# Pairs' matrix products from seven products of halves instead of eight, with weights in rings of quarters

## The chip, the cores and the metric

The kernel runs on one core of a Trainium2 chip. The metric is the device time of one launch in microseconds. The program works with five engines that run their own instruction streams: TensorE (PE; its weight loads are shown apart as PEld), VectorE (DVE), ScalarE (ACT), GpSimd (POOL) and SyncE (SP), and with DMA queues. Order between engines comes from semaphore waits that the framework puts in for every true dependence, overwriting included.

## The reference

A block of cross attention between 512 tokens and 32 state rows is followed by a mixture of 8 experts with top-1 routing. Input: `x` (8, 8, 512, 64) and `state` (8, 8, 32, 64); after attention, 8 x 544 = 4352 rows of width 512.

```python
# attention: x reads the states, the states read x, both softmaxed
xread = softmax(scale * x @ state.T) @ state
sread = softmax(scale * state @ x.T) @ x
rows  = concat([xread, sread], axis=2)         # -> (8, 544, 512)
# routing, row by row of one batch
fresh_e = argmax(rows @ w_gate)
e = fresh_e if s == 0 or sigmoid(rows @ w_local) < 0.5 else prev_e
p = softmax(rows @ w_gate)
# expert e of 8: w1 is 512 x 1024, w2 is 1024 x 512
h = maximum(row @ w1[e], 0)
out = p[e] * (h @ w2[e])
```

All of it is float32.

## The kernel before

The program has three stages: attention (class `Attention`), routing (class `Routing`), and the experts (function `experts`, from line 745). The change is in the last one, with small edits to what the routing allocates.

Routing sorts the rows by expert. Every expert's rows are cut into *pairs* of 2 x 128 rows (`PAIR` = 256), and what is left of each expert into *tiles* of 32 rows. With the inputs of this case there are 16 pairs and 10 tiles. How many there are is known only at run time; at least 10 pairs exist whatever the data (`NPMIN`), so the first nine calls of `pair` stand in straight code, and from the tenth on each pair asks in a branch (function `last`, line 937) whether another follows. Pairs 0 to 9 each carry one tile along (`tiles[u]`), the later ones none.

A pair u does this (function `pair`, line 859):

- SyncE loads the weights of pair u+1: `load`, four pieces of 1 MB, halves of w1 into `a` and of w2 into `c`. Both exist twice and are used in turn (line 752).
- VectorE turns the rows of pair u+1 (`turned`, line 778: two block transposes of 128 x 512 from `xg` into `xt`), GpSimd fetches those of pair u+2 (`gather`, line 767: eight indirect DMAs of quarter rows).
- First layer: for pairs from 1 on, 8 blocks of 128 hidden units by 4 steps of the 512-wide sum, each a matmul with a 128 x 128 block of w1 held in the array and 256 columns of rows streamed (line 875). ScalarE takes each full PSUM bank through the ReLU into `h` (line 877). Pair 0 does the same for 128 rows at a time, so its matmuls stream 128 columns (line 886).
- `tile.one` (line 832): the tile's first layer, 32 rows held and 256 columns of w1 streamed at a time, ReLU on ScalarE, transpose on VectorE.
- `after.load(0)` and `after.gather`: w1 of the next tile into `at`, its rows.
- Second layer, for each 128 rows: 8 matmuls with a block of `h` held and 512 columns of w2 streamed (line 902). VectorE multiplies by the rows' probability into `y` (line 906) and GpSimd scatters `y` into `out` with an indirect DMA (line 908).
- `tile.two` (line 845): the tile's second layer, scaled on VectorE (854), scattered by GpSimd (856). Then `after.load(1)`: w2 of the next tile into `ct`, and `after.turned`.

The order of the work is the order of the code (`tc.manual_schedule`): every engine and every queue runs its instructions in the order in which the calls above issue them, and waits where a dependence is open. SyncE's queue holds all weight loads, so a load that waits for its buffer holds back the loads behind it. GpSimd's queue holds gathers and scatters. [...]

Of the kernel before, what the change touches and what calls it, by code (L numbers as in the profile page):

```python
# [18 lines left out]
P = 128  # L19
# [30 lines left out]
def kernel(  # L50
# [24 lines left out]

    nc = tc.nc
# [29 lines left out]
    with ExitStack() as phase:  # L106
        bank = banks(phase, 7)
        route.route(bank, phase, lt, slots)
        experts(phase, tc, bank, w1, w2, rows, slots, route, out)
# [344 lines left out]
class Routing:  # L454
# [79 lines left out]
    def route(self, bank, ctx, lt, slots):  # L534
# [3 lines left out]
        idle = ctx.enter_context(self.tc.tile_pool(name="idle", bufs=1, space=PSUM)).tile([P, 512], F32, name="idle")  # L538

        def keep(n):  # L540

            for i in range(n):
                nc.tensor.matmul(idle, lhsT=identb, rhs=place.rearrange("p k c -> p (k c)"),
                                 start=True, stop=True)
# [123 lines left out]
        bc = rt.tile([P, 2, NG, NBLK, CG], BF16, name="bc")  # L668
# [48 lines left out]
        def probabilities():  # L717
# [3 lines left out]
            pb = rt.tile([P, 3, NG, NBLK, CG], BF16, name="pb")  # L721
# [23 lines left out]
def experts(ctx, tc, bank, w1, w2, rows, slots, route, out):  # L745
# [3 lines left out]
    hp = ctx.enter_context(tc.tile_pool(name="hp", bufs=2))  # L749


    as_ = [[fx.tile([P, KT, F // 2], F32, name=f"a{i}{h}") for h in range(2)] for i in range(2)]
    cs_ = [[fx.tile([P, FK // 2, D], F32, name=f"c{i}{h}") for h in range(2)] for i in range(2)]
    at_ = fx.tile([P, KT, F], F32, name="at")
    ct_ = fx.tile([P, FK, D], F32, name="ct")
    xts_ = [fx.tile([P, KT, PAIR], F32, name=f"xt{i}") for i in range(2)]
# [3 lines left out]
    first = [fx.tile([P, D], F32, name=f"first{b}") for b in range(2)]  # L760
# [17 lines left out]
    def turned(u):  # L778
        for b in range(2):
            x_t = xts_[u % 2][:, :, b * P:b * P + P]  # L780
            if u:
                nc.vector.transpose(x_t.rearrange("p k (i t) -> p k i t", i=Q),  # L782
                                    xgs_[u % 2][:, b].rearrange("p i k t -> p k i t"))
                continue

            for h, copy in enumerate((nc.vector.tensor_copy, nc.scalar.copy)):
# [4 lines left out]
                copy(x_t[:, 2 * h:2 * h + 2, :], t.rearrange("p (k t) -> p k t", k=KT // 2))  # L791
# [5 lines left out]
    def load(u, parts=range(4)):  # L797
        e = index(slots.experts[0:1, u - 1:u] if u else slots.expert if 0 in parts else slots.again)
        for i in parts:
            to, w = ((as_, w1), (cs_, w2))[i // 2]  # L800
            to, w = to[u % 2][i % 2], w[bass.ds(e, 1), i % 2]
            if u == 0 and i < 2:
                chunks = w.rearrange("o (q x) (k f) -> (o x) k q f", q=Q, k=KT)
                for j in range(KT):
                    nc.sync.dma_start(out=to[SQ * j:SQ * j + SQ], in_=chunks[:, j])
# [3 lines left out]
    class Tile:  # L809
# [12 lines left out]
        def load(self, of):  # L822
            e = index(slots.experts[0:1, NP - 1 + self.i:NP + self.i])
            for half in range(2):
# [3 lines left out]
                else:  # L828
                    to = ct_[:, half * FK // 2:(half + 1) * FK // 2, :].rearrange("p m d -> p (m d)")
                    nc.sync.dma_start(out=to, in_=w2[bass.ds(e, 1), half].rearrange("o p x -> (o p) x"))  # L830
# [14 lines left out]
        def two(self):  # L845

            yps = bank(P, P)
            for m in range(FK):
                for g in range(Q):
                    nc.tensor.matmul(yps[SQ * g:SQ * g + SQ, :], lhsT=self.h[:, m, :], rhs=ct_[:, m, g * P:g * P + P],  # L850
# [7 lines left out]

    def pair(u, ahead=True, tile=None, after=None):

        a, c, x_t = as_[u % 2], cs_[u % 2], xts_[u % 2]
        if ahead:
            load(u + 1)
            if u:
                turned(u + 1)
        if ahead and u and u + 2 < NP:
            gather(u + 2)
        h = hp.tile([P, FK, PAIR], F32, name="h")
        if u:
            for n in range(4):  # L870
                hps = bank()
                for i in range(2):
                    f = (2 * n + i) % 4 * P
# [123 lines left out]
```

## Time and profile before

| | us |
|---|---|
| median of 10 runs (629.26 to 632.7) | 630.65 |
| the profiled execution | 630.79 |
| its span, first to last instruction | 629.0 |
| TensorE busy | 583.8 (93%) |
| VectorE busy | 155.2 (25%) |
| ScalarE busy | 95.6 (15%) |
| GpSimd busy | 217.4 (35%) |
| mean granted TensorE clock of the core | 0.974 |

The experts' stage starts at 125.7 us, where pair 0's first matmul runs, and TensorE's last matmul ends at 614.2. In the timeline a line is: start, length, engine, line of the kernel, operation, what it writes <- what it reads, count, and in brackets how long the engine sat idle before it and who ended that. A busy TensorE is modelled from the matmuls' ends, so two starts that lie apart by a whole group are the better measure of what a group costs. "PEld" is the loading of the held operand, which overlaps the matmuls. In a group's row, the first number behind the bar is the time in which at least one of its instructions ran, the second the mean length of one in ns; lengths overlap.

### The profile page before, as it was taken

To read this page: it belongs to the slowest core of one execution; us is meant where nothing else is said; L and a number is where in the kernel's file an instruction comes from. 1 tells how busy PE (TensorE), PEld (TensorE's weight loads), DVE (VectorE), ACT (ScalarE), POOL (GpSimd) and SP (SyncE) were. 2 spreads that over 40 slices of the span, in tenths; PEclk is the share of its full clock that TensorE was granted. 3 is DMA by queue.
4 is the path that set the end of the run, shared out by engine and by line. 5 is a ranking of instruction groups with operands and counts; after the bars stand their busy time and mean duration, and the time that the engine had idled before them with its cause. 6 is when DMAs were issued, how large, how long until landed. Compare 5 with 4: busy or idle time off the path is not lost. (4 is left out here: it accounts for less than half of the span.)

```text
span 629.0 us, 9298 instructions
## 1 busy us (share of the span) xinstructions
PE 583.8 (93%) x3760; PEld 379.8 (60%) x3763; DVE 155.2 (25%) x335; ACT 95.6 (15%) x190; POOL 217.4 (35%) x218
## 2 busy tenths in 40 slices
PE   7678776799999999999999999999999999999990
PEld 3455552495757575757575766666667585766750
DVE  4698988721101010101010101010101011010000
ACT  5446531210010101010101010101011010101100
POOL 4333430373151616151515151516154151433000
PEclk9889997799999999999999999999999999999996
DMA  8968732699995969695959595959597355550000
GB/s 321 410 217 290 264 142 93 153 350 403 351 374 226 383 227 384 216 392 213 395 207 395 209 398 208 395 205 398 208 408 263 133 222 192 207 181 23 35 21 20
DMA packets 43227, 159.35 MB, mean 253 GB/s; under 512 B 8049, under 2 KB 8177, under 8 KB 31394
## 3 DMA queue, kind: packets, MB, share of 16 engines
q1 hardware_dynamic: 35682, 140.04, 59.7%
q0 software_dynamic: 7488, 18.56, 8.2%
q8 instruction: 35, 0.57, 0.4%
q14 instruction: 22, 0.18, 0.1%
HBM read 140.74 MB, written 17.96 MB: 252 GB/s over the span
## 5 line engine op out<-in xcount | busy, mean ns | idle before, releaser
L902 PE MATMUL ps<-c,h 128*128 128x512 f32 x512 | 223.4, 594 | 0.0
L875 PE MATMUL ps<-xt,a 128*128 128x256 f32 x960 | 210.7, 380 | 0.0
L875 PEld LDWEIGHTS ps<-xt,a 128*128 128x128 f32 x960 | 181.6, 190 | 28.4 <-issue 4.4
L902 PEld LDWEIGHTS ps<-c,h 128*128 128x128 f32 x512 | 96.5, 190 | 119.2 <-issue 118.7
L764 POOL DMA_INDIRECT xg<-rows,row x128 | 124.8, 975 | 39.0 <-issue 38.1
L908 POOL DMA_INDIRECT out_dram<-y,tok x32 | 32.2, 1008 | 201.5 <-DVE y L906 195.7
L877 ACT ACTIVATE h<-ps 128x512 f32<-128x512 f32 x60 | 35.8, 597 | 402.1 <-PE ps L875 402.1
L906 DVE TENSOR_SCALAR y<-ps,prob 128x512 f32<-128x512 f32 x32 | 24.0, 751 | 272.3 <-PE ps L902 272.3
L436 PE MATMUL v<-sd,a 128*128 128x265 f32 x128 | 34.7, 405 | 12.6 <-ACT xr L439 9.0
L843 DVE STREAM_TRANSPOSE htt<-ht 128x256 f32<-128x256 f32 x10 | 4.5, 445 | 132.4 <-ACT ht L841 132.4
L436 PEld LDWEIGHTS v<-sd,a 128*128 128x128 f32 x128 | 22.4, 189 | 23.2 <-ACT xr L439 15.1
L856 POOL DMA_INDIRECT out_dram<-yt,row x10 | 9.8, 981 | 73.3 <-issue 73.3
L387 POOL TENSOR_TENSOR e<-e,z 128x1024 f32<-128x1024 f32 x8 | 15.3, 1912 | 28.2 <-DVE z L386 28.2
L375 POOL TENSOR_TENSOR e<-e,m 128x1024 f32<-128x1024 f32 x8 | 15.3, 1912 | 17.5 <-DVE m L374 17.5
L850 PEld LDWEIGHTS ps<-ct,htt 128*32 128x32 f32 x640 | 16.9, 110 | 6.9 <-issue 6.8
L850 PE MATMUL ps<-ct,htt 128*32 128x128 f32 x640 | 19.5, 274 | 0.0
L838 PE MATMUL ps<-at,xtt 128*32 128x256 f32 x320 | 19.3, 382 | 0.0
L782 DVE STREAM_TRANSPOSE xt<-xg 128x512 f32<-128x512 f32 x30 | 19.1, 674 | 0.0
L886 PE MATMUL ps<-xt,a 128*128 128x128 f32 x128 | 14.5, 276 | 0.6 <-DVE experts L720 0.6
L344 PE MATMUL s<-x_t,sttc 64*32 64x512 f32 x128 | 12.7, 715 | 2.5 <-issue 2.1
L886 PEld LDWEIGHTS ps<-xt,a 128*128 128x128 f32 x128 | 14.4, 192 | 0.8 <-DVE again L719 0.8
L838 PEld LDWEIGHTS ps<-at,xtt 128*32 128x32 f32 x320 | 9.4, 109 | 8.4 <-issue 3.3
(178 smaller groups left out, 301.3 us busy)
## 6 DMA issues: line engine op xcount, KB each, us to landing
c<-in_w_dram SPq DMA_DIRECT2D x32, 1024.0 KB, 17.2
a<-in_w_dram SPq DMA_DIRECT2D x30, 1024.0 KB, 10.3
at<-in_w_dram SPq DMA_DIRECT2D x22, 1024.0 KB, 7.6
ct<-in_w_dram SPq DMA_DIRECT2D x22, 1024.0 KB, 8.6
x_t<-in_xt_dram SPq DMA_DIRECT2D x16, 512.0 KB, 7.1
x_n<-in_xn_dram SPq DMA_DIRECT2D x8, 1024.0 KB, 8.2
rows<-xr SPq DMA_DIRECT2D x8, 1024.0 KB, 5.7
a<-in_w_dram SPq DMA_DIRECT2D x8, 256.0 KB, 7.6
```

The source lines that it names most:

```text
L375: nc.gpsimd.tensor_tensor(e1, e1, m1.to_broadcast([P, A, N]), op=Alu.subtract)
L436: nc.tensor.matmul(v[:, u, :VW], lhsT=self.a[:, u, c * P:c * P + P], rhs=at.sd[:, b, u * VW:(u + 1) * VW], start=True, stop=True)
L764: nc.gpsimd.indirect_dma_start(out=to.rearrange("p k t -> p (k t)"), out_offset=None, in_=rows.rearrange("n q x -> (n q) x"), in_offset=ba ...
L782: nc.vector.transpose(x_t.rearrange("p k (i t) -> p k i t", i=Q), xgs_[u % 2][:, b].rearrange("p i k t -> p k i t"))
L838: nc.tensor.matmul(hps[SQ * g:SQ * g + SQ, :], lhsT=self.x_t[:, j, :], rhs=a[:, j, :, g], start=(j == 0), stop=(j == KT - 1))
L850: nc.tensor.matmul(yps[SQ * g:SQ * g + SQ, :], lhsT=self.h[:, m, :], rhs=ct_[:, m, g * P:g * P + P], start=(m == 0), stop=(m == FK - 1))
L875: nc.tensor.matmul(hps[:, i * PAIR:(i + 1) * PAIR], lhsT=a[n // 2][:, j, f:f + P], rhs=x_t[:, j, :], start=(j == 0), stop=(j == KT - 1))
L877: nc.scalar.activation(h[:, 2 * n:2 * n + 2, :].rearrange("p m t -> p (m t)"), hps, Act.Relu)
L886: nc.tensor.matmul(hps[:, i * P:i * P + P], lhsT=a[n][:, j, i * P:i * P + P], rhs=x_t[:, j, of], start=(j == 0), stop=(j == KT - 1))
L902: nc.tensor.matmul(yps, lhsT=h[:, m, b * P:b * P + P], rhs=c[m // 4][:, m % 4, :], start=(m == 0), stop=(m == FK - 1))
L906: nc.vector.tensor_scalar(y, yps, slots.prob[:, k:k + 1], None, Alu.mult)
L908: nc.gpsimd.indirect_dma_start(out=out, out_offset=to, in_=y, in_offset=None, bounds_check=NT - 1, oob_is_err=False)
```

## The change

For pairs from 1 on, both layers are cut into 2 x 2 blocks, and each layer's eight block products become seven (Strassen's algorithm in Winograd's form), with sums of blocks before and after. Written for weights a (blocks a11, a12, a21, a22) and rows b:

- `first_sums` and `second_sums` make three sums of weight blocks in free ring slots and overwrite a fourth block (a21, or w2's b12) with a fourth sum: four additions of 128 x 1024 on VectorE for each layer. `column_sums` makes four sums of the rows' blocks (128 x 256).
- `seven` issues the products in the order 1, 5, 6, 2, 7, 3, 4. The product 1 goes into a rotating bank `x`; ScalarE copies it into a bank of its own, `y` (one of the two `sums`), and the products 6, 7 and 4 add to that bank by further matmuls without a new start. Product 2 adds to `x`, product 3 to `v`, where 5 stands. Between the products ScalarE takes the partial sums out to SBUF (`s5, s2, s7`; in the second layer `r5, r2, r7`, scaled by the rows' probability), and VectorE adds them up.
- The first layer's results stay as four blocks (`h11, h21, c12, h22`), and VectorE makes the four sums that the second layer's products need from them (`hs`, and `c12` in place).
- A product of the first layer is 8 matmuls with 128 x 128 held and 128 columns streamed; one of the second layer is 4 matmuls with 256 columns streamed.

Weights lie in two rings of nine slots of 512 KB (`ring`), one for w1 and one for w2; a pair takes seven slots of each, four for quarters and three for sums, and the next pair's quarters begin in the two slots behind them. So of the four quarters of a layer two are loaded at the start of the pair before, and two after its product 2, where `others` issues them. w2 is laid out by quarters in DRAM on the host (a reshape of the input). Rows have one buffer `x_t` instead of two; the sums and the transpose for the next pair (`ready`) are issued after product 2 of the second layer.

Pair 0 (`plain`) keeps its products, with the second layer in halves of 256 columns. The first pair's w1 is loaded in 16 pieces instead of 8. The tile's transpose moves from the end of a pair to the start of the next, behind `second_sums`. The rotating banks are six, and the routing's `keep` matmuls go to the two `sums` banks in turn. The loads ahead of pair 0 are issued in the order w2 of pair 0, `at`, w1 of pair 1, `ct`, w2 of pair 1.

```diff
-        bank = banks(phase, 7)
+        bank = banks(phase, 6)
+        sums = phase.enter_context(tc.tile_pool(name="sums", bufs=1, space=PSUM))
+        sums = [sums.tile([P, 512], F32, name=f"sum{i}") for i in range(2)]
...
+    RING = 9
+    ring = [[fx.tile([P, KT // 2, F // 2], F32, name=f"a{i}") for i in range(RING)],
+            [fx.tile([P, FK // 2, D // 2], F32, name=f"c{i}") for i in range(RING)]]
...
+    first = [fx.tile([P, D], F32, name=f"y{b}") for b in range(2)]
+    ys = first
+    xs = [fx.tile([P, KT // 2, P], F32, name=f"xs{i}") for i in range(4)]
+    hs = [fx.tile([P, FK // 2, P], F32, name=f"hs{i}") for i in range(3)]
+    h11, h21, c12, h22 = hqs = [fx.tile([P, FK // 2, P], F32, name=f"h{i}") for i in range(4)]
+
+    def places(u, i):
+        n = 7 * u - 3 if u else 0
+        (w11, w12, w21, w22), sums = [[ring[i][(n + j) % RING] for j in js] for js in (range(4), range(4, 7))]
+        return ((w11, w12), (w21, w22)) if i == 0 else ((w11, w21), (w12, w22)), sums
...
+    def load(u, i, quarters=slice(4)):
+        e = index(slots.experts[0:1, u - 1:u] if u else slots.again if i else slots.expert)
+        q = places(u, i)[0]
+        for half, other in [((0, 0), (0, 1), (1, 0), (1, 1)), ((0, 0), (1, 0), (0, 1), (1, 1))][i][quarters]:
+            to = q[half][other]
...
+            if u == 0 and i == 0:
...
+                    nc.sync.dma_start(out=to[SQ * j:SQ * j + SQ], in_=chunks[:, j, 2 * other:2 * other + 2])
...
+    def add(out, a, b, op=Alu.add):
+        nc.vector.tensor_tensor(out, a, b, op=op)
+
+    def sums_of_rows(x, to, third):
+        (b11, b12), (b21, b22) = x
+        add(to[0], b12, b11, Alu.subtract)
+        add(to[1], b22, to[0], Alu.subtract)
+        third(b22, b12)
+        add(to[2], b21, to[1], Alu.subtract)
+
+    xq = [[x_t[:, 2 * j:2 * j + 2, t * P:t * P + P] for t in range(2)] for j in range(2)]
+
+    def first_sums(u, part):
+        ((a11, a12), (a21, a22)), to = places(u, 0)
+        if part == 0:
+            add(to[0], a21, a22)
+            add(to[1], to[0], a11, Alu.subtract)
+        else:
+            add(a21, a11, a21, Alu.subtract)
+            add(to[2], a12, to[1], Alu.subtract)
+
+    def column_sums():
+        sums_of_rows(xq, (xs[0], xs[1], xs[3]), lambda b22, b12: add(xs[2], b22, b12, Alu.subtract))
+
+    def second_sums(u):
+        sums_of_rows(*places(u, 1), lambda b22, b12: add(b12, b12, b22, Alu.subtract))
+
+    def seven(y, n, product, copies, whole):
+        x, v = bank()[:, :n], bank()[:, :n]
+        y = y[:, :n]
+        product(x, 1, True)
+        nc.scalar.copy(y, x)
+        product(v, 5, True)
+        five, two, three = copies
+        five(v)
+        product(y, 6)
+        two(y)
+        product(x, 2)
+        whole(1, x)
+        product(y, 7)
+        three(y)
+        whole(4, None)
+        product(v, 3)
+        whole(2, v)
+        product(y, 4)
+        whole(3, y)
...
+    def strassen(u, others, between, ready):
...
+        firsts = {1: (a11, b11), 2: (a12, b21), 3: (was[2], b22), 4: (a22, xs[3]), 5: (was[0], xs[0]),
+                  6: (was[1], xs[1]), 7: (a21, xs[2])}
+        s5, s2, s7 = [h1.tile([P, FK // 2, P], F32, name=f"s{i}") for i in range(3)]
...
+        def first(to, i, begin=False):
+            w, x = firsts[i]
+            for m in range(FK // 2):
+                for j in range(KT // 2):
+                    nc.tensor.matmul(to[:, m * P:m * P + P], lhsT=w[:, j, m * P:m * P + P], rhs=x[:, j, :], ...)
+
+        def first_whole(i, t):
+            if i == 1:
+                others(0)
+                nc.scalar.activation(flat(h11), t, Act.Relu)
+            elif i == 4:
+                add(flat(h22), flat(s7), flat(s5))
+                nc.scalar.activation(flat(h22), flat(h22), Act.Relu)
+            elif i == 2:
+                add(flat(c12), t, flat(s2))
+                nc.vector.scalar_tensor_tensor(hs[0], c12, 0.0, h22, Alu.max, Alu.add)
+                add(hs[1], hs[0], h11, Alu.subtract)
+                nc.vector.scalar_tensor_tensor(c12, c12, 0.0, h11, Alu.max, Alu.subtract)
+            else:
+                nc.scalar.activation(flat(h21), t, Act.Relu)
+                add(hs[2], h21, hs[1], Alu.subtract)
...
+        between()
...
+        seconds = {1: (h11, d11), 2: (h21, d21), 3: (hs[2], d22), 4: (h22, wcs[2]), 5: (hs[0], wcs[0]),
+                   6: (hs[1], wcs[1]), 7: (c12, d12)}
...
+        def second_whole(i, t):
+            if i == 1:
+                others(1)
+                scaled(ys[0][:, low], p0)(t)
+                ready()
+            elif i == 4:
+                add(ys[1][:, high], r7, r5)
+            elif i == 2:
+                nc.vector.scalar_tensor_tensor(ys[0][:, high], t, p0, r2, Alu.mult, Alu.add)
+                scatter(2 * u, ys[0])
+            else:
+                scaled(ys[1][:, low], p1)(t)
+                scatter(2 * u + 1, ys[1])
...
+    def pair(u, ahead=True, tile=None, after=None):
+        if u:
+            if ahead:
+                for i in range(2):
+                    load(u + 1, i, slice(2))
+                if u + 2 < NP:
+                    gather(u + 2)
+            second_sums(u)
+            if tile:
+                tile.turned()
+
+        def between():
+            if u == 0:
+                next(route.probabilities)
+            if tile:
+                tile.one()
+            if after:
+                after.load(0)
+                after.gather()
+            if u == 0:
+                gather(2)
+
+        def others(i):
+            if ahead:
+                load(u + 1, i, slice(2, 4))
+
+        def ready():
+            if ahead:
+                first_sums(u + 1, 0)
+                turned(u + 1)
+                column_sums()
+                first_sums(u + 1, 1)
+
+        if u:
+            strassen(u, others, between, ready)
+        else:
+            plain(u, between, ready)
...
         if tile:
             tile.two()
         if after:
             after.load(1)
-            after.turned()
...
-    load(0, range(2, 4))
-    for of in range(2):
-        tiles[0].load(of)
+    load(0, 1)
+    tiles[0].load(0)
+    load(1, 0)
+    tiles[0].load(1)
+    load(1, 1)
```

138 lines of the change are left out of this document (66 added, 72 removed).

## Prediction

> **What bounds the kernel now.** I read the page from the top, then the groups, then TensorE's timeline, then each stage's window, and only then the queues that the change touches.
>
> ```profile
> span 629.0 us, 9298 instructions
> PE 583.8 (93%) x3760; PEld 379.8 (60%) x3763; DVE 155.2 (25%) x335; ACT 95.6 (15%) x190; POOL 217.4 (35%) x218
> PE   7678776799999999999999999999999999999990
> ```
>
> TensorE is full in every slice from the ninth on, which is the experts' stage. The groups and the timeline tell what one pair costs; first pair 0, whose first layer streams 128 columns at a time, then the others.
>
> ```profile
> L875 PE MATMUL ps<-xt,a 128*128 128x256 f32 x960 | 210.7, 380 | 0.0
> L886 PE MATMUL ps<-xt,a 128*128 128x128 f32 x128 | 14.5, 276 | 0.6 <-DVE experts L720 0.6
> L886 PEld LDWEIGHTS ps<-xt,a 128*128 128x128 f32 x128 | 14.4, 192 | 0.8 <-DVE again L719 0.8
> ```
>
> ```profile
> 125.72 14.53 PE L886 MATMUL ps<-xt,a 128*128 128x128 f32 x128 [0.61 <-DVE experts L720]
> 140.09 5.67 PE L687 MATMUL ps<-pb,inp 128*128 128x150 bf16 x40
> ```
>
> ```profile
> 416.98 14.08 PE L875 MATMUL ps<-xt,a 128*128 128x256 f32 x64
> 430.99 1.93 PE L838 MATMUL ps<-at,xtt 128*32 128x256 f32 x32
> 432.86 14.00 PE L902 MATMUL ps<-c,h 128*128 128x512 f32 x32
> 446.79 1.96 PE L850 MATMUL ps<-ct,htt 128*32 128x128 f32 x64
> 448.67 14.08 PE L875 MATMUL ps<-xt,a 128*128 128x256 f32 x64
> ...
> 476.32 13.98 PE L875 MATMUL ps<-xt,a 128*128 128x256 f32 x64
> 490.14 13.90 PE L902 MATMUL ps<-c,h 128*128 128x512 f32 x32
> 503.87 13.98 PE L875 MATMUL ps<-xt,a 128*128 128x256 f32 x64
> ```
>
> Each float32 matmul of the code is two passes in the trace (32 matmuls, x64). Group L875 holds 960/64 = 15 pairs, u = 1 to 15. Nine of them carry a tile of 32 tokens and take 448.67 - 416.98 = 31.69 us; the six later ones take 503.87 - 476.32 = 27.55: 13.82 for the first layer, 215.9 ns a pass of 256 columns, and 13.73 for the second, 429.1 ns a pass of 512. In these six nothing idles between the groups. So the stage is bound by the columns that TensorE streams.
>
> ```profile
> 125.70:140.20 14.50, 14.47 (x129) 14.50 (x130) 3.33 (x4) 1.79 (x3) 11.55 (x10) 1.00 0.94 344
> 163.50:177.50 14.00, 14.00 (x72) 12.07 (x68) 1.76 (x4) 1.79 (x3) 4.94 (x6) 1.00 0.98 382
> 478.00:506.00 28.00, 28.00 (x99) 18.64 (x99) 3.17 (x5) 2.39 (x4) 10.09 (x11) 1.00 0.53 189
> ```
>
> In these windows (columns: length, busy PE, PEld, DVE, ACT, POOL, clock, DMA share, GB/s) the granted clock is 1.00, so there is no clock to win or lose. Vector works 3 us of 28 and Scalar 2.4: room for additions.
>
> **The change, part by part.** *Products.* A first-layer product of halves is 4 x 2 matmuls of 128 columns, 16 passes; a second-layer one is 4 matmuls of 256 columns, 8 passes. Seven of each make 112 passes of 128 and 56 of 256. For the second I take 215.9 ns: 12.09 us. For the first the right row is pair 0, which already streams 128 columns with a fresh weight tile each time: (140.09 - 125.72)/128 = 112.3 ns, so 12.58 us and 1.80 us a product. Below that lies half of the 256-wide pass, 108.0 ns; above, the L886 group's own 14.5/128 = 113.3. A pair falls from 27.55 to 24.67 us, by 2.88; fifteen give **-43.2 us**, with 2.77 to 3.37 a pair from the two ends, -41.5 to -50.5. Pair 0 keeps its eight products; its second layer becomes 64 passes of 256, 13.82 us against 13.73, nothing.
>
> *Additions.* Their prices:
>
> ```profile
> L391 DVE STREAM_TRANSPOSE a<-e 128x1024 f32<-128x1024 f32 x8 | 9.7, 1209 | 0.0
> L637 DVE TENSOR_TENSOR at<-at,less 128x320 f32<-128x320 f32 x1 | 0.5, 470 | 0.0
> L681 DVE TENSOR_TENSOR inp<-place,pos 128x1024 bf16<-128x1024 bf16 x4 | 2.5, 685 | 0.0
> L375 POOL TENSOR_TENSOR e<-e,m 128x1024 f32<-128x1024 f32 x8 | 15.3, 1912 | 17.5 <-DVE m L374 17.5
> L791 DVE COPY xt<-ps 128x256 f32<-128x256 f32 x2 | 0.8, 425 | 1.4 <-PE ps L790 1.4
> L782 DVE STREAM_TRANSPOSE xt<-xg 128x512 f32<-128x512 f32 x30 | 19.1, 674 | 0.0
> L877 ACT ACTIVATE h<-ps 128x512 f32<-128x512 f32 x60 | 35.8, 597 | 402.1 <-PE ps L875 402.1
> ```
>
> No row is a float32 add of 1024 on Vector. The bfloat16 one (0.69) lies below, GpSimd's float32 one (1.91) above. The transposes give 535 ns for 512 elements more, so 0.47 us at 320 becomes 1.2 at 1024; I take that. 512 elements cost 0.7, 256 cost 0.43. Per pair: eight weight sums, 9.6; four column sums, 1.7; six steps on the first layer's results, 4.2; two on the second's, 0.9; the transposes as before, 1.3; together 17.7 us, a tile's three steps 1.1 more. That is 72% of 24.67 (at 1.91 an add it would be 23.4, 95%). Scalar gets seven moves of 512 (0.6) and six of 256 (taken as 0.43 too): 6.8 us. Both fit under TensorE, if their results come in time.
>
> Do they? The order is 1, 5, 6, 2, 7, 3, 4. The first bank is copied while product 5 runs (0.6 us and a handover against 1.80), and each later copy has a product between it and the matmul that adds to the same bank. The second layer's product 5 needs the sum made from product 3: three Vector steps, 2.1 us, against product 4, 1.80, and product 1, 1.73. The sums for the next pair (the calls in `ready`) stand in Vector's queue behind the last first-layer step, at about 14 us of a pair, and take 7.9 (four adds, transposes, column sums): done at 22, or 23 in a tile pair, where TensorE wants them at 24.7 and 28.8. `second_sums` then takes 4.8 and is wanted 12.6 later. Between products waits are added, 14 a pair, but satisfied ones cost nothing in the rows: 490.14 - 476.32 is exactly 64 passes with three groups' boundaries inside. If they were not satisfied, TensorE itself would stand.
>
> *Moved.* A tile's transpose (0.3 us on Vector) goes from the end of a pair to behind `second_sums`, 7 us before `tile.one` wants it; `gather(2)` moves within GpSimd's queue from before to behind a tile's gather, wanted a pair later. Of six banks instead of seven a pair takes two for each layer and two for its tile, so each comes round a pair later. All three: nothing, and about their own length if uncovered.
>
> *Weights.* The bytes stay. Half of the next pair's quarters go into slots free since the pair before; the other half are issued at product 2 of each layer, after Sync's earlier waits: `ct` behind `tile.two`, `at` behind `tile.one`.
>
> ```profile
> a<-in_w_dram SPq DMA_DIRECT2D x30, 1024.0 KB, 10.3
> xg<-rows,row POOLq DMA_INDIRECT x128, 5.7
> out_dram<-y,tok POOLq DMA_INDIRECT x32, 4.0
> ```
>
> A tile pair moves 8.4 MB of weights and 1 MB of rows; at the 382 GB/s of the row 163.50:177.50 that is 24.6 us of 28.8. The first layer's late quarters, issued 7.2 us into the pair behind 4.2 MB, land at about 14 to 15, just when `ready` asks; 5 us of slack follow, and a landing of 10.3 from issue, as now, would cost 3 of them. The first pair's weights leave in 16 pieces instead of 8:
>
> ```profile
> 107.20 4.38 SPq L805 DMA_DIRECT2D a<-in_w_dram  x8
> a<-in_w_dram SPq DMA_DIRECT2D x8, 256.0 KB, 7.6
> ```
>
> 16 pieces issue in twice 4.38 us, until 116, and at 7.6 to landing are there at 123.6, before 125.72. I cost it at nothing: the routing on Vector hides it. Were that gone, the second eight issues would show, 4.4 us.
>
> *GpSimd's queue and the end.*
>
> ```profile
> 125.64 3.40 DVE L723 TENSOR_TENSOR pb<-inb,parts 128x2000 bf16<-128x2000 bf16 x3
> 125.90 3.96 POOL L764 DMA_INDIRECT xg<-rows,row  x1 [0.30 <-issue]
> 130.16 0.94 POOL L764 DMA_INDIRECT xg<-rows,row  x1 [0.30 <-issue]
> ```
>
> That is a gather beside three additions, for rival (a). Next, how scatters follow each other, and the last one:
>
> ```profile
> 162.62 1.00 POOL L908 DMA_INDIRECT out_dram<-y,tok  x1 [5.85 <-DVE probq L737]
> 163.60 0.35 DVE L854 TENSOR_SCALAR yt<-ps,probq 128x128 f32<-128x128 f32 x1 [0.62 <-PE ps L850]
> 171.41 0.98 POOL L856 DMA_INDIRECT out_dram<-yt,row  x1 [7.79 <-issue]
> ```
>
> ```profile
> 614.26 0.75 DVE L906 TENSOR_SCALAR y<-ps,prob 128x512 f32<-128x512 f32 x1 [6.06 <-PE ps L902]
> 615.29 0.98 POOL L908 DMA_INDIRECT out_dram<-y,tok  x1 [5.83 <-DVE y L906]
> ```
>
> `yt` is ready at 163.95, yet its scatter starts at 171.41: scatters into `out` wait for the landing of the one before. Until now 16 passes of 429.1 ns, 6.9 us, lay between a pair's two scatters; now they come one product apart, 1.73 us, so the second waits for the first's landing, 4.0. Inside the run that is hidden; at the very end it is not: about **+2 us**.
>
> *Sum.* Against the profiled execution's own 630.8 us (span 629.0, and 1.8 around it): 630.8 - 43.2 + 2 = **590 us**. The runs' median, 630.65, differs by 0.1.
>
> **The rivals.** (a) *Queues lag*: GpSimd's cycle in a tile pair is scatter 1.0, landing 4.0, scatter 1.3, wait 7.8, scatter 1.3, nine gathers at 1.24: 26.6 us of 28.8. The rows at 125.64 and 125.90 show a gather of 0.94 taking 3.96, until three two-input additions in a row had ended. Vector now runs such adds for 15 us a pair. Rows gathered 22 us into a pair have landed at 28 (5.7) and are wanted 14 us into the next, at 43. If two us a pair are lost, these 15 us are gone after eight pairs, and `ready` waits for rows: one us on each of 14 pairs is 604 us. The same time comes from late quarters or from 0.07 us at each boundary.
>
> [...] If every gather and scatter stands until no add runs, the cycle grows from 26.6 by the blocked part. Beyond 31.7 - 26.6 = 5.1 us the nine tile pairs lose; the six others win 17.3, less the 2 at the end, so the kernel is slower from 5.1 + 15.3/9 = 6.8 us on. Half of the 15 us, 7.5, gives 630.8 + 9 x 2.4 - 15.3 = 637 us. For it: the 3.96. Against: that gather ended 0.82 us after the adds, so it needs them gone only at its start, and most sums here depend on the one before, which leaves a gap. [...]
>
> (c) *Nothing won*: a boundary costs 0.2 us, as from L902 to L850 in the tile pairs (446.79 - 432.86 = 13.93 against 13.73). 14 x 0.2 x 15 = 42 us: 632. Against: the tile changes the operand's shape, a product does not.
>
> (d) *Narrow products cost more*: the weight load is not hidden. A load takes 192 ns in the L886 rows; if each pass took that, the first layer would be 112 x 192 = 21.5 us, each pair 7.7 - 1.64 = 6.0 us longer, the kernel 724 us. Against: the same rows, where load and pass together keep 112.3. [...]
>
> (e) *More won*: weight loads wholly hidden, 108.0 ns: 582 us.
>
> **How the numbers follow.** The forecast has 0.61, its own range 585 to 597; (a) 0.21; (b) 0.07; (c) 0.04, one half of it within 0.2%; (d) 0.02; (e) 0.05. About 0.2% is what a measurement of this kernel can tell from no change. Faster: 0.61 + 0.21 + 0.05 + 0.01 = 0.88; same 0.02; slower 0.10. The range goes from (e) to somewhat above (a), 582 to 612, and leaves out (b), (c), (d) and a part of (a): 0.18.
>
> **What would show it.** Right: 112 passes of 128 columns near 112 ns and 56 of 256 near 216 per pair; tileless pairs 24.7 us apart, tile pairs 28.8; clock 1.00; Vector near 70% in the stage. Wrong, by step: TensorE idle before a product, released by Scalar (copies) or by Vector (sums); Vector idle on `xg` or on a weight quarter, for (a); gathers of 2 us and more, scatters drifting later from pair to pair, for (b); passes of 128 columns well over 112 ns for (d). A last scatter more than 4 us behind the last product would unmake the end's term.

## The result, and the profile after

The changed kernel takes **592.63 us** (median of nine executions, 591.07 to 597.89) against 630.61 of the kernel before (629.09 to 632.7), a ratio of 0.940 with a 95% interval of [0.939, 0.942]. The forecast was 590 us. That holds for the chips of the result and of the first four experiments. On another chip, that of r9 to r12, the same kernel lost; on the chip of r5 to r8 only edited forms of it ran, and they all took longer than the kernel before. Both are told below, the gain first.

The profiled execution of the changed kernel took 592.38 us. From its page, the span, the engines' busy time and TensorE's row of slices:

```profile
span 590.5 us, 12467 instructions
PE 540.7 (92%) x4872; PEld 461.5 (78%) x4875; DVE 368.0 (62%) x605; ACT 163.0 (28%) x325; POOL 236.2 (40%) x218
PE   7688877799999999999999999999999999999960
```

TensorE is as full as before and has 43.1 us less to do (583.8 before). Vector went from 155 to 368 us of work and Scalar from 96 to 163, and neither shows in TensorE's row. TensorE's timeline of the first pair with products of halves, a tile pair (start, duration, line, operands, passes):

```profile
163.44 2.05 PE L950 MATMUL ps<-xt,a 128*128 128x128 f32 x16
165.32 1.95 PE L950 MATMUL ps<-xs,a 128*128 128x128 f32 x16
167.11 1.95 PE L950 MATMUL sum<-xs,a 128*128 128x128 f32 x16
...
176.14 1.93 PE L859 MATMUL ps<-at,xtt 128*32 128x256 f32 x32
...
179.83 1.89 PE L983 MATMUL ps<-c,hs 128*128 128x256 f32 x8
181.56 1.89 PE L983 MATMUL sum<-c,hs 128*128 128x256 f32 x8
...
190.28 1.96 PE L871 MATMUL ps<-ct,htt 128*32 128x128 f32 x64
192.17 2.05 PE L950 MATMUL ps<-xt,a 128*128 128x128 f32 x16
...
446.74 1.95 PE L950 MATMUL ps<-xt,a 128*128 128x128 f32 x16
...
471.33 1.95 PE L950 MATMUL ps<-xt,a 128*128 128x128 f32 x16
```

No row has an idle time in brackets. A first-layer product follows the last after 1.79 us (167.11 - 165.32), 111.7 ns a pass; a second-layer one after 1.73 us (181.56 - 179.83), 215.9 ns a pass. Seven and seven, with the tile's 1.9 and 1.9, make 192.17 - 163.44 = 28.73 us (31.69 before); a tileless pair takes 471.33 - 446.74 = 24.59 (27.55 before). One stall stands between 163 and 570 us, at the start of the last pair, and the other news is at the end. The timeline there, all engines:

```profile
546.13 2.02 PE L950 MATMUL ps<-xt,a 128*128 128x128 f32 x16 [0.85 <-DVE c L882]
...
569.07 1.89 PE L983 MATMUL sum<-c,h 128*128 128x256 f32 x8
...
570.53 0.98 POOL L933 DMA_INDIRECT out_dram<-y,tok  x1 [19.34 <-DVE y L997]
571.00 0.47 ACT L987 ACTIVATE y<-sum,prob 128x256 f32<-128x256 f32 x1 [2.98 <-PE sum L983]
576.46 0.98 POOL L933 DMA_INDIRECT out_dram<-y,tok  x1 [4.95 <-ACTq L1110]
```

The last product begins at 569.07 and takes 1.73 us, so TensorE ends at 570.8. By the same measure it ended at 614.05 before (600.32, the start of its last group, and 32 passes of 429.1 ns; 614.2 is the modelled end), so it ends 43.3 us earlier. The second half of `y` is ready at 571.47, and its scatter starts 5 us after that: 4.95 us behind the end of the first scatter's issue. The last scatter thus stands 5.7 us behind TensorE's end (576.46 - 570.8) where it stood 1.2 behind before (615.29 - 614.05). So the books are: -43.3 at TensorE's end, +4.4 between it and the last scatter, and 14.0 us from there to the end of the span (13.7 before), +0.3. The sum is -38.5 with the rounding, which is 629.0 less 590.5.

The windows show the clock and the load of a tile pair, of a tileless pair, and of all pairs but the first and last (columns as in the prediction):

```profile
192.20:220.90 28.70, 28.70 (x268) 25.73 (x264) 17.82 (x25) 7.26 (x14) 13.16 (x12) 1.00 0.89 327
446.70:471.30 24.60, 24.60 (x169) 23.15 (x169) 20.08 (x27) 6.87 (x13) 10.65 (x11) 1.00 0.64 211
163.50:546.10 382.60, 381.78 (x3217) 347.45 (x3217) 247.42 (x338) 99.69 (x191) 171.88 (x159) 1.00 0.83 300
```

Vector is busy for 247.42 of 382.6 us, 65%; the granted clock is 1.00.

### The profile page after: what moved, and what is told of

Same layout as the page of the kernel before. It is cut to its first block, busy times and chain, and to the rows that moved or that the text cites. A ratio compares the mean times of both kernels' runs of the same rounds, so it can differ in the third digit from the quotient of the medians.

```text
span 590.5 us, 12467 instructions
## 1 busy us (share of the span) xinstructions
PE 540.7 (92%) x4872; PEld 461.5 (78%) x4875; DVE 368.0 (62%) x605; ACT 163.0 (28%) x325; POOL 236.2 (40%) x218
## 4 chain that ended last, share of the span: by engine, by line
PE 75%; DMA 10%; DVE 4%; ACT 3%; issue 2%; POOL 2%; SPq 2%; DVEq 0%; ACTq 0%
PE ps L950 17%; PE ps L983 16%; PE sum L950 13%; PE sum L983 11%; DMA xg<-rows,row 7%; PE ps L871 3%; PE ps L859 3%; PE v L440 3%; PE ps L1013 2%; PE ps L1022 2%; POOL e L379 2%; PE sum L546 1%; ACT xr L443 1%; DMA wgs<-in_wg_dram 1%; SPq L826 1%
## 5 line engine op out<-in xcount | busy, mean ns | idle before, releaser
L950 PE MATMUL ps<-xt,a 128*128 128x128 f32 x720 | 88.8, 277 | 0.9 <-DVE c L882 0.9
L950 PE MATMUL sum<-xs,a 128*128 128x128 f32 x720 | 87.8, 275 | 0.0
L950 PEld LDWEIGHTS ps<-xt,a 128*128 128x128 f32 x720 | 84.3, 192 | 3.4 <-issue 3.2
L882 DVE TENSOR_TENSOR a<-a,a 128x1024 f32<-128x1024 f32 x60 | 72.0, 1220 | 21.6 <-DMA a<-in_w_dram 20.3
L950 PEld LDWEIGHTS sum<-xs,a 128*128 128x128 f32 x720 | 84.0, 192 | 0.0
L882 DVE TENSOR_TENSOR c<-c,c 128x1024 f32<-128x1024 f32 x60 | 70.7, 1220 | 1.0 <-DMA c<-in_w_dram 0.3
L983 PE MATMUL ps<-c,h 128*128 128x256 f32 x240 | 57.6, 383 | 0.0
L983 PE MATMUL ps<-c,hs 128*128 128x256 f32 x240 | 56.7, 379 | 0.0
L983 PE MATMUL sum<-c,h 128*128 128x256 f32 x240 | 56.7, 379 | 0.0
L882 DVE TENSOR_TENSOR h<-s,s 128x512 f32<-128x512 f32 x15 | 10.5, 698 | 73.0 <-ACT s L971 73.0
L983 PEld LDWEIGHTS ps<-c,h 128*128 128x128 f32 x240 | 44.4, 190 | 9.1 <-issue 3.7
L440 PEld LDWEIGHTS v<-sd,a 128*128 128x128 f32 x128 | 22.7, 192 | 22.9 <-ACT xr L443 14.9
L878 POOL DMA_INDIRECT out_dram<-yt,row x10 | 10.8, 1076 | 70.3 <-issue 49.6
## 6 DMA issues: line engine op xcount, KB each, us to landing
a<-in_w_dram SPq DMA_DIRECT2D x60, 512.0 KB, 13.8
```

The lines of the kernel that those rows point to most:

```text
L440: nc.tensor.matmul(v[:, u, :VW], lhsT=self.a[:, u, c * P:c * P + P], rhs=at.sd[:, b, u * VW:(u + 1) * VW], start=True, stop=True)
L882: nc.vector.tensor_tensor(out, a, b, op=op)
L950: nc.tensor.matmul(to[:, m * P:m * P + P], lhsT=w[:, j, m * P:m * P + P], rhs=x[:, j, :], start=begin and m == 0 and j == 0, stop=(m == FK ...
L983: nc.tensor.matmul(to, lhsT=x[:, m, :], rhs=w[:, m, :], start=begin and m == 0, stop=(m == FK // 2 - 1), skip_group_check=True)
```

## The experiments

Runs r1 to r4 were made on one chip, r5 to r8 on a second and r9 to r12 on a third. Times are compared inside these sets, except where r9 is set against the result.

**r1: the changed kernel again.** 

> The changed kernel once more, as the base for the three others that run beside it: 592.6 us, 0.940 of the kernel before.

594.01 us (592.12 to 598.9), 0.943 of the kernel before beside it, [0.940, 0.946]. This is the base for r2 to r4.

**r2: the last pair's second scatter left out.**

```
             scaled(ys[1][:, low], p1)(t)
-            scatter(2 * u + 1, ys[1])
+            if ahead:                      # not in the last pair
+                scatter(2 * u + 1, ys[1])
```

> Leaves out the scatter of the last pair's second 128 rows (they stay unwritten). My theory: the end is long because this scatter waits 4.95 us for the landing of the one before it; without it the whole end moves up by that wait and the scatter's own 0.98, so 586.5 us. Rival: the end is set by what follows the pairs (the tile's transpose at 578.03 us and the branch of `rest`), and the scatter only stands in front of it; then the time stays within 1 us of 592.6.

587.38 us (585.68 to 592.94), 0.933 [0.930, 0.936], 6.6 us under r1. The rival, by which the end hangs on what follows the pairs, falls: the tile's transpose, which starts at 578.03 us in the result and 579.03 in r1, comes at 570.32. Not all of the 6.6 belongs to the edit: in the traced execution the pairs' first matmul already stands at 123.45 us, where r1 has it at 125.65. Measured inside the traces, the span ends 14.9 us behind TensorE's end in r2 and 20.5 behind it in r1, so the scatter costs 5.6 us there; my theory had 5.9.

**r3: the last pair's second layer with eight products, one block of 128 rows after the other.**

```
+        if not ahead:
+            for b, hb in enumerate(((h11, h21), (c12, h22))):
+                yps = bank()
+                ...            # 32 passes of 256 columns for 128 rows
+                nc.vector.tensor_scalar(ys[b], yps, (p0, p1)[b], None, Alu.mult)
+                scatter(2 * u + b, ys[b])
+            return
```

> The last pair's second layer with eight products of halves, first all for its first 128 rows, then all for the others; all else as changed. 64 passes of 215.9 ns instead of 56: TensorE ends 1.7 us later. The two scatters then stand 6.9 us apart, more than the first needs to land, and the last one starts about 1 us behind the last product as it did before the change, instead of 5.7. My theory: +1.7 - 4.7 = -3.0, so 589.6 us. Rival (the end hangs on what follows the pairs): +1.7, so 594.3.

589.76 us (588.07 to 590.42), 0.934 [0.932, 0.937], 4.3 us under r1. The timeline of r1, and then of r3, at the end:

```profile
570.74 0.98 POOL L933 DMA_INDIRECT out_dram<-y,tok  x1 [18.93 <-DVE y L997]
577.47 0.98 POOL L933 DMA_INDIRECT out_dram<-y,tok  x1 [5.75 <-ACTq L1110]
```

```profile
558.87 13.98 PE L1012 MATMUL ps<-c,h 128*128 128x256 f32 x64
...
567.01 0.98 POOL L933 DMA_INDIRECT out_dram<-y,tok  x1 [15.92 <-DVE y L1015]
...
573.92 0.98 POOL L933 DMA_INDIRECT out_dram<-y,tok  x1 [5.92 <-DVE y L1015]
```

In r3 the second scatter waits for Vector's `y` and no longer for the scatter before it. TensorE does eight products instead of seven, 1.7 us more, and the last scatter still comes 3.6 us earlier than in r1; the start of the last pair is the same (546.29 and 546.34).

**r4: the order 1, 5, 6, 2, 3, 7, 4 in the last pair.**

```
+        if early:                          # the last pair's second layer
+            product(v, 3); whole(2, v)     # first 128 rows are whole
+            product(y, 7); three(y); whole(4, None)
+            product(x, 4, True); whole(5, x)   # Vector adds r7 to it
+            return
```

> In the last pair's second layer the order 1, 5, 6, 2, 3, 7, 4 instead of 1, 5, 6, 2, 7, 3, 4, with product 4 in a bank of its own, so that the first 128 rows are done two products ahead of the others and not one. The first scatter starts 1.73 us earlier and the second waits for it as before. My theory: -1.7, so 590.9 us. Rival (the end hangs on what follows the pairs): 592.6.

588.85 us (588.35 to 590.06), 0.934 [0.932, 0.936], 5.2 us under r1. From its timeline:

```profile
566.95 0.98 POOL L942 DMA_INDIRECT out_dram<-y,tok  x1 [17.80 <-DVE y L1006]
567.15 1.89 PE L992 MATMUL ps<-c,h 128*128 128x256 f32 x8
...
571.96 0.98 POOL L942 DMA_INDIRECT out_dram<-y,tok  x1 [4.03 <-issue]
```

The second scatter still waits for the first, 4.03 us, but the first now starts before the last product does. TensorE ends at 568.9, the last scatter stands 3.1 us behind it, 3.4 less than r1's 6.5. I had expected 1.7; the rest of these 3.4 is the landing, 4.03 here and 5.75 in r1. Another 2 us of r4's gain come from ahead of the pairs (first matmul at 123.68 against 125.65), and nothing in the edit explains them. Either way r3 and r4 both beat the changed kernel, by under 1%: their intervals (up to 0.937 and 0.936) end below r1's (from 0.940).

**r5: the first layer with eight products, the late quarters asked for early.**

```
-        seven(sums[0], 512, first, [...], first_whole)
+        for i, t, to in ((0, 0, h11), (1, 1, h22), (0, 1, c12), (1, 0, h21)):
+            ...                # 32 passes of 128 columns
+            if to is h11:
+                others(0)
```

> The first layer of pairs 1 to 15 with eight products of halves in the same narrow form (128 passes of 128 columns instead of 112), and none of its eight sums on Vector (four weight sums, four of rows); the second layer as changed. My theory: TensorE's passes are all that counts and the sums are hidden, so each pair is 16 passes of 111.6 ns longer, 1.79 us: tileless pairs 26.4, tile pairs 30.5 apart, the kernel 592.4 + 26.8 = 619 us. [...]

759.78 us; the kernel before took 642.27 beside it. Its question stays open here: `others(0)`, the load of the next pair's late quarters, stands ahead of products that read those slots, so part of the first layer is computed with the next pair's weights and has to wait for them. r10 has the load behind the products that read the slots.

**r6 and r7: ten and twenty more additions on Vector.**

```
                 first_sums(u + 1, 1)
+                for _ in range(10 if u else 0):     # r7: 20
+                    add(spare, spare, spare)        # 128 x 320
```

> Ten more additions of 320 elements on Vector behind the sums of each pair from 1 on (some 0.48 us each, 4.8 us a pair, results unused). Vector then works about 22.3 us of 24.6 in a tileless pair, 23.4 of 28.7 in a tile pair. My theory: still hidden, within 1.5 us of 592.6. Rival: additions on Vector hold up GpSimd's gathers and scatters; they then grow from 1.08 us on average to 1.3 or more and the kernel by 5 us or more.

> Twenty such additions a pair, 9.6 us. Vector then has 27.1 us of work in a tileless pair, where TensorE has 24.6, and 28.2 in a tile pair, where TensorE has 28.7. My theory: Vector becomes the bound in the six tileless pairs only, 2.5 us each: 604 to 610 us. Rival (GpSimd held up by additions): the tile pairs grow too, by 2 us and more each, and the time is above 620.

With ten additions 668.72 us (a second execution took 700.8), with twenty 659.4 us (657.77 and 661.03), beside 642.27 of the kernel before. Twenty additions took less time than ten, which fits neither theory.

**r8: product 6 directly behind product 1.**

```
+        if n == 512:
+            product(y, 6); two(y)
+            product(v, 5, True); five(v)
```

> In the first layer of pairs 1 to 15 the products' order 1, 6, 5, 2, 7, 3, 4 instead of 1, 5, 6, 2, 7, 3, 4: product 6 adds to the bank that Scalar fills with a copy of product 1, and nothing runs between. My theory: TensorE then stands while the copy is made, 0.35 us from its last pass to the copy's start, 0.5 of copy, 0.2 until the next matmul: 1.1 us in each of 15 pairs, so 609 us. Rival: a boundary costs 0.2 us, as between the second layer and a tile: 595.6 us.

708.39 us beside 642.27. The expected waits are there, 0.66 us and 0.71 us in the first two pairs, but the run is some 100 us longer than they make. With that, four edits that have little in common had all come out far too long, on a chip on which the kernel before also took 11 us more than elsewhere. What was missing was the changed kernel itself on such a chip.

**r9: the changed kernel on such a chip.** 

> The changed kernel beside the three below. In the last four runs (on another chip than the first four) engines stood for up to 8 us where the profile shows nothing that they wait for, in every one of the four edits, and the kernel before itself took 642 us. Theory A: the stalls belong to that chip; the changed kernel stalls there too, and takes 650 us or more; on the chip of the first runs it takes 592.6 as before. Theory B: the stalls come from the edits; the changed kernel takes 0.940 of the kernel before on either chip.

677.94 us (674.15 to 682.22) against 642.37 (640.62 to 644.51) of the kernel before: **1.054** [1.049, 1.059]. This is a third chip, and the kernel before is as slow on it as on the second. Theory A holds on it: here the change costs 5%, with no edit at all. (On the second chip the changed kernel was never run unedited.) Its page, the span and the rows of TensorE and of the granted clock; behind them the clock row of the result's execution:

```profile
span 680.4 us, 12470 instructions
PE   7678777959999898969696978969799998797980
PEclk8999997969999799979798998979799999989995
```

```profile
PEclk8989999789999999999999999999999999999995
```

TensorE now has a hole in most pairs, and with it a stretch of lower clock. r9's timeline shows the first hole, in pair 0, whose first layer is the same code in both kernels; with it GpSimd's gathers:

```profile
135.66 0.94 POOL L780 DMA_INDIRECT xgt<-rows,row  x1 [0.30 <-issue]
...
137.88 0.49 PE L1013 MATMUL ps<-xt,a 128*128 128x128 f32 x3 [0.54 <-issue]
...
145.65 0.94 POOL L780 DMA_INDIRECT xg<-rows,row  x1 [0.30 <-issue]
146.38 0.37 PE L1013 MATMUL ps<-xt,a 128*128 128x128 f32 x1 [1.73 <-issue]
147.78 0.37 PE L1013 MATMUL ps<-xt,a 128*128 128x128 f32 x1 [1.03 <-issue]
149.19 1.44 PE L1013 MATMUL ps<-xt,a 128*128 128x128 f32 x6 [1.04 <-issue]
```

From 137 us on, TensorE starts a few passes at a time, at distances of 0.7, 1.4 and 2.1 us, and waits for nothing that the profile shows. It began while GpSimd issued gathers back to back, one each 1.25 us (they had run for 12 us by then), and ended 3.5 us behind the start of the last of them. Pair 0 takes 48.96 us to the next pair's start, where the result's execution takes 37.82. In the pairs that follow the hole comes again, here in pair 9:

```profile
475.28 1.99 PE L983 MATMUL ps<-c,h 128*128 128x256 f32 x8
476.34 0.95 POOL L780 DMA_INDIRECT xg<-rows,row  x1 [0.30 <-issue]
477.11 1.89 PE L983 MATMUL ps<-c,hs 128*128 128x256 f32 x8
...
482.59 0.94 POOL L780 DMA_INDIRECT xgt<-rows,row  x1 [0.30 <-issue]
...
483.29 7.54 SPq L828 DMA_DIRECT2D c<-in_w_dram  x2
483.30 0.36 ACT L915 COPY sum<-ps 128x256 f32<-128x256 f32 x1 [4.82 <-issue]
...
483.70 3.78 PE L983 MATMUL sum<-c,hs 128*128 128x256 f32 x8 [4.70 <-issue]
...
487.28 3.19 PE L983 MATMUL ps<-c,h 128*128 128x256 f32 x8
```

Here TensorE stands 4.7 us until the last gather is out, and the two products behind take 3.6 and 3.0 us instead of 1.73: the granted clock is 0.50 from 483.7 to 487.2 us. It isn't TensorE alone that stands. The product behind the hole adds to the bank into which Scalar copies product 1, and it starts right behind that copy. The product behind product 1 begins at 477.11, and in the result's execution the copy starts 0.2 us behind that point (208.77 against 208.57 in pair 2). Here it starts 6.2 us behind it, at 483.30, and SyncE's next load, into a slot that product 1 read, at 483.29. Over the whole run this is most of the holes:

```profile
PE sum L983 <- ACT sum L915: 43.6, 10, 6.6
```

Why both start so late, no row tells, nor whether product 1 was done when the records of its passes say so. I added up the distances between the starts of neighbouring passes as far as they exceed 0.44 us, where they are over 0.6: after 126 us they make 59 us in r9, and 58 of them lie between the first gather of a pair and 2.5 us behind its last, stretches that make up 40% of the time from there to TensorE's end. In the result's execution the same sum is 0.8 us, with the same gathers. To the 59 come ten stretches of 3.4 to 10.2 us at half clock between 140 us and TensorE's end, 65 us in all, in which TensorE loses up to 32. Together they are as much as the 90 us by which r9's span exceeds the result's (680.4 against 590.5).

**r10: the first layer with eight products, the late quarters asked for behind the fourth.**

```
+        for i, t, to in ((0, 0, h11), (0, 1, c12), (1, 1, h22), (1, 0, h21)):
+            ...
+            if to is c12:
+                others(0)
```

> The first layer of pairs 1 to 15 with eight products of halves in the same narrow form (128 passes of 128 columns instead of 112), without its eight sums on Vector; the late quarters of the next pair are asked for behind the fourth product, as in the changed kernel. My theory: the sums are hidden and TensorE's passes count alone, so 1.79 us a pair, 15 pairs, 26.8 us above the changed kernel beside it (619 where that takes 592.6). Rival: the sums cost something, and part of the 26.8 comes back: below 24 us.

711.23 us (710.91 to 713.35), 33.3 above r9; the traced executions lie 28.9 apart (spans of 709.3 and 680.4). Neither is under 24, which speaks against the rival: dropping four weight sums and four row sums a pair gave nothing back that can be seen. But both kernels have holes (the same count gives 56 us here), and r11 below shows that work on Vector moves them by more than the few us in question, so the total alone doesn't decide it. What does is the result's own trace, where TensorE stands nowhere in pairs 1 to 14 with all the sums in place. Inside a pair without a hole in its first layer the timeline has

```profile
400.00 14.56 PE L975 MATMUL ps<-xt,a 128*128 128x128 f32 x128
414.49 1.93 PE L859 MATMUL ps<-at,xtt 128*32 128x256 f32 x31
```

14.49 us for 128 passes, where the changed kernel's 112 take 12.70 (176.14 - 163.44): 1.79 for the eighth product, as expected.

**r11: twenty additions beside r9.** 

> Twenty more additions of 320 elements a pair on Vector, 9.6 us. My theory: Vector's 27.1 us become the bound in the six tileless pairs, 2.5 us each, and the tile pairs stay as they are: 12 to 18 us above the changed kernel beside it. Rival (additions hold GpSimd's gathers and scatters up): the tile pairs grow by 2 us and more too, 30 us or more in all, and gathers take 1.3 us and more.

655.46 us (653.05 to 664.32), 22.5 *below* r9. Both theories fail on the total. The row of r11's gathers on GpSimd, and then its timeline in pair 2:

```profile
L782 POOL DMA_INDIRECT xg<-rows,row x128 | 146.6, 1145 | 39.0 <-issue 36.9
```

```profile
232.82 1.19 POOL L782 DMA_INDIRECT xg<-rows,row  x1 [0.30 <-issue]
...
240.00 0.45 PE L873 MATMUL ps<-ct,htt 128*32 128x128 f32 x6 [0.31 <-issue]
...
242.91 1.86 PE L952 MATMUL ps<-xt,a 128*128 128x128 f32 x11 [0.24 <-issue]
243.41 0.94 POOL L782 DMA_INDIRECT xgt<-rows,row  x1 [0.30 <-issue]
```

A gather takes 1.15 us here and 1.02 in r9, so beside more additions gathers took 0.13 us longer, an eighth, and not the length of an addition (0.47 us at 320 elements, L637 in the kernel before). The additions also moved the whole burst of gathers, in most tile pairs from some 11 us into the pair to 20 or later, and TensorE's stops moved with it: in pair 2 they stand in the tile's second layer (L873) and at the next pair's start, short and 0.7 us apart, and no longer in the second layer's first products. The same count of distances gives 24 us instead of 59, 23 of them beside gathers, and the half clock takes 24 us up to TensorE's end instead of 65. Whether Vector's 27 us bind in tileless pairs can't be read from this run.

**r12: product 6 directly behind product 1, beside r9.** 

> The first layer's products in the order 1, 6, 5, 2, 7, 3, 4, so that nothing runs while Scalar copies product 1 into the bank that product 6 adds to. In the run on the other chip TensorE waited 0.66 to 0.71 us for this copy in each of 15 pairs. My theory: these waits are all that the order costs, 15 x 0.7 = 10.5 us above the changed kernel beside it (I had taken 1.1 us a pair before). Rival: 0.2 us at each boundary, 3 us in all.

688.75 us (median of three, 687.73 to 693.73; a fourth execution took 707.44), 10.8 above r9. Its waits of TensorE (sum, times, longest):

```profile
PE sum L989 <- ACT sum L915: 40.6, 12, 6.5
PE sum L956 <- ACT sum L915: 10.7, 15, 0.7
```

The second row is the edit: 15 waits of 0.7 us for Scalar's copy, 10.7 us, and the rival's 3 falls. That the total agrees to 0.1 us is luck, since r9 itself varies by 8 us. The first row is the hole of r9 again. So a copy of 512 columns that has no product to hide behind costs 0.7 us, and the order of products in the change hides 30 copies of this kind, two in each of 15 pairs (the second layer's are of 256 columns, and what they would cost was not measured).

## Why the prediction was right, and where it was not

*Products* (forecast -43.2): right, in its pieces too. Passes of 128 columns went at 111.7 ns (forecast 112.3), of 256 at 215.9 (215.9); pairs stand 24.59 and 28.73 us apart (24.67 and 28.8). TensorE's end moved by 43.3 us: 44.4 by the pairs, less 1.0 that the last pair starts late and 0.1 in its first product. That this comes so close to 43.2 is in part luck: the pairs gained 1.2 us more than forecast, and a stall that was not foreseen took 1.0. Of rival (d) no more was seen than the 3.4% by which 111.7 exceeds 108.0, half of the 256-wide pass.

*Additions*: the price was right. The row of the weight sums on Vector, with its waits:

```profile
L882 DVE TENSOR_TENSOR a<-a,a 128x1024 f32<-128x1024 f32 x60 | 72.0, 1220 | 21.6 <-DMA a<-in_w_dram 20.3
a<-in_w_dram SPq DMA_DIRECT2D x60, 512.0 KB, 13.8
```

1.22 us against 1.2. Vector was busy for 65% of the stage (forecast near 70). What was wrong is *when* the late quarters come. The second row has 13.8 us from issue to landing, a median over early and late quarters together (r1 has 9.6). Vector waited 20.3 us for the late ones in all, in pairs 0 to 10: `ready` began some 17 us into the pairs 1 to 9 instead of 14, and 18.5 us into pair 10, with the longest wait, 4.06. That took most of the slack which the prediction put at 5 us, and TensorE lost nothing by it, because the sums that come last are wanted only by the products 3 and 7.

*Moved steps, weights in 16 pieces*: nothing, as forecast. Pair 0 starts at 125.62 us (125.72 before); the pieces landed after 3.9 us.

*GpSimd's queue*: gathers take 1.08 us (0.98 before), with no lag from pair to pair; from pair 1 on the longest took 1.99. A tenth more fits rival (a) and rival (b), by which every gather and scatter stands until no addition runs, at a small part of the size that they needed: 2 us a pair for (a), more than 6.8 for (b). r11, with more additions and 1.15 us against r9's 1.02, fits it too. That the additions are the cause was not shown.

*Boundaries*, rival (c): none had a wait. r12 shows what one costs when it has: 0.7 us.

**The step that failed is the end's term, "about +2 us"**: it was +4.4. The mechanism was the one named, and r2, r3 and r4 show it by taking the second scatter away, apart, or forward. The size was off because the working set the landing, 4.0, the median before, against the distance of the two scatters, 1.73; but the median landing of these scatters is 7.3 us after the change, and at the end the first scatter starts 1.46 us behind the end of product 3 (570.53 against 569.07), is issued for 0.98, and the second then waited 4.95 for it here, 5.75 in r1. 1.46 + 0.98 + 4.95 less the last product's 1.73 is the 5.7 between TensorE's end and the second scatter, and 1.2 of these were there before. The forecast's own sign of this, a last scatter more than 4 us behind the last product, is what the trace shows.

*Not foreseen*: the 1.0 us at the last pair's start, and that the result depends on the chip. On r9's chip the time, 677.94 us, is far outside the range of 582 to 612; that the forecast was put to the test on a chip where TensorE has no such gaps (0.8 us of them in the result's execution, 59 in r9's) is luck. All rows of the prediction came from one trace, and no rival asked what happens to twice as many, half as long passes where TensorE has them.

## What to carry to other kernels

Price a product by the trace's own rows of the same width and type, count what each replaced product must have copied or summed beside it, and order the products so that each copy has one to hide behind (without one it cost 0.7 us in r12); then seven products in place of eight take 24.59 us in place of 27.55, 10.7% less, where an eighth would be 12.5%. Look at the end of the program apart: work that is hidden in every other round shows there, and two scatters into one tensor want more distance than the first one's landing (here the second waited 4.03 to 5.75 us for it). Time such a change on more than one chip: this one gained 6% on one and lost 5% on another, with the same code.

## What the runs showed of the hardware

- **On some chips engines were held up by something that the profile has no row for.** On the chips of r5 to r12 TensorE started a few passes at a time, or stood for up to 6.6 us (r9) until a copy that Scalar began late was done, while GpSimd issued gathers (r9: 58 of 59 us of such gaps; they moved with the gathers in r11). With the same gathers the sum of such gaps is 0.8 us in the result's execution, and from 400 to 560 us r1 to r4 have one wait of TensorE each, at the last pair's start. That the gathers are the cause is not shown: the late quarters' transfers run in the same stretch. The changed kernel issues passes nearly twice as often (168 in 24.59 us of a tileless pair, 96 in 27.55 before); but of r9's eight gaps of 4 us and more, seven have no packet on the queues of the kind `instruction`, and the eighth has one of 16 KB, so no run shows that instructions were waited for. The traces of those chips also lack the landing times of all transfers, so a difference in recording can't be excluded. The kernel before was timed but not traced there; that it lost 11.7 us and pair 0's hole alone costs 11.1 fits that its longer passes are spared, and is argued, not shown.
- **In r9 a hole cost twice.** A stretch of half clock, 3.4 to 10.2 us, begins in most holes and outlasts them: two products behind one took 3.6 and 3.0 us instead of 1.73, at a granted clock of 0.50.
- **The landing of a scatter of 128 rows varied.** At the end, where DMA moves 58 GB/s (the result, 571 to 576.4 us; 270 over its span), the next scatter waited 4.03, 4.95 and 5.75 us (r4, the result, r1). Over all 32 of them the median from issue to landing is 7.3 us in the result and 4.0 before.
- **The last pair starts 1 us late; what causes it is not shown.** The last pair, alone in an `Else`, starts 1.0 us late in the result (546.13, where the product ahead of it began at 543.39 and takes 1.73) and 1.0 to 1.4 in r1 to r4; the six pairs ahead, in `If` bodies, lose nothing. The row at 546.13 names a weight sum of w2 (`c`, L882) as what ended the wait, but r3 leaves these sums out of the last pair and is 1.1 us late all the same. The kernel before has the same `Else` and no gap there (586.51). A queue of the kind `instruction` moved 16 KB at 543.6 us in the result, 2.5 us ahead of the last pair's first pass, and at 579.9 and 583.3 in the kernel before, 6.6 and 3.2 us ahead of it; that these packets are TensorE's, or have to do with the wait, is a guess.
